# One DRAIN of GpSimd between the output scatters of a fused attention, MoE and routed-expert kernel

## The chip, the cores and the metric

The kernel runs on one core of a Trainium2 chip. The metric is the device time of one execution in microseconds; shown are the median of three runs and one profiled execution of the same program.

## The reference

Three stages follow each other, all in float32. The attention has 4 batches of 8 heads, 576 positions and 64 columns per head, with a bias made of a running sum. Its output, 2304 rows of 512, goes through a dense layer whose hidden value is the largest of three products. The last stage routes each row to one of 8 experts and writes the row of the result:

```python
    e_idx = np.argmax(logits, axis=1)
    ...
    for e in range(E):
        mask = e_idx == e
        ...
        h = np.maximum(x[mask] @ w1[e], 0.0)
        out[mask] = gate_w[mask, None] * (h @ w2[e])
```

## The kernel before

The change touches only the last stage, the routed experts. Its rows are cut into units of up to 256 rows of one expert. There are ten units in a fixed order, numbered 0 to 9 by `n` in the loop at line 811; unit 9 has 128 rows at most. Behind them stand eleven more units inside nested `tc.If(n_u > n)` (line 835 and on), which run only when the experts' row counts ask for them; with these inputs none does.

For each unit the weights of its expert are loaded by SyncE (`weights`), the rows are gathered by GpSimd with an indirect DMA (`gather`), turned and multiplied by TensorE (`transposed`, `stage_1`), and multiplied again 128 rows at a time (`stage_2(u, 0)` and `stage_2(u, 1)`). `stage_2` ends with ScalarE writing the scaled rows to `y` and GpSimd scattering them to their places in the output by an indirect DMA (line 661). Each such scatter writes the whole tensor `out` as the program sees it, so each waits until the one before has landed. Ten units make 19 scatters.

GpSimd issues four kinds of DMA in the whole program: the split of weights (line 127), the routing table's entries (line 506), the gathers (line 578) and the scatters (line 661).

Behind the last unit every engine loads the number of further units (line 832), branches past the nested blocks (line 833), and meets the others in the program's closing steps, which the profile puts on line 889. There GpSimd has a semaphore instruction for the blocks that were jumped over (INC_SWDGE_SEM), then a DRAIN, then a barrier that all five engines share, a clearing of semaphores and a second barrier. Each engine has DRAINs of its own in these closing steps, and each has one more at the program's start (line 882).

The order of instructions on each engine is set by a scheduler when the program is built. `tc.keep_in_program_order` holds an instruction at the place where the code has it.

Of the kernel before, what the change touches and what calls it, by code (L numbers as in the profile page):

```python
# [47 lines left out]
N_EARLY = 4  # L48

T_PE = T_EARLY  # L50
NU_STATIC = 5
# [34 lines left out]
def fused_kernel(tc, qk, vd, sd, w64, mod, wg, wgt, mb, we, cst, csi, out):  # L86
    nc = tc.nc
    V, A, G, P, SP = nc.vector, nc.scalar, nc.gpsimd, nc.tensor, nc.sync
    top = ExitStack()
    with top:  # L90
# [60 lines left out]
        with ExitStack() as es:  # L151
# [248 lines left out]
            for p in range(1, NP):  # L400
# [17 lines left out]
                if p % (H // 2) == H // 2 - 1:  # L418
                    b = PORD[p] // (H // 2)
                    n = 0  # L420
# [163 lines left out]
        def weights(u, n, which, raws):  # L584
            pools = SETS[(2 * n + which) % 3]
            hs, ls = [], []
            for g in range(4):
                pool, tag = pools[g]
                raw = raws[g % len(raws)].tile([128, 2, 512], F32, tag="raw", name="e_raw")
                SP.dma_start(out=raw.rearrange("p a n -> p (a n)"), in_=we[bass.ds(u["e"], 1), which * 4 + g].rearrange("e p n -> p (e n)"))  # L590
                for a in range(2):
                    h = pool.tile([128, 512], F32R, tag=tag, name="e_h")
                    lo = pool.tile([128, 512], F32R, tag=tag, name="e_l")
                    A.copy(out=h, in_=raw[:, a])  # L594
                    V.tensor_tensor(out=lo, in0=raw[:, a], in1=h.bitcast(F32), op=ALU.subtract)  # L595
                    hs.append(h)
                    ls.append(lo)
            u[which] = hs, ls

        def transposed(u):  # L600
            u["x"] = xt = xbp.tile([128, 2, 4, UNIT], F32R, tag="xb", name="x2t")[:, :, :, 0:u["n"]]
            for a in range(2):
                x_ps = ps_a.tile([128, 512], F32, tag="a", name="x_ps").rearrange("p (c n) -> p c n", c=2)[:, :, 0:u["n"]]
                for c in range(2):
                    for i in range(u["n"] // 128):
                        k = 2 * a + c
                        P.transpose(out=x_ps[:, c, i * 128:(i + 1) * 128], in_=u["g"][:, i, k * 128:(k + 1) * 128], identity=ident)
                A.copy(out=xt[:, 0, 2 * a:2 * a + 2], in_=x_ps)
                V.tensor_tensor(out=xt[:, 1, 2 * a:2 * a + 2], in0=x_ps, in1=xt.bitcast(F32)[:, 0, 2 * a:2 * a + 2], op=ALU.subtract)
# [41 lines left out]
        def stage_2(u, i):  # L651
            hs, ls = u[1]
            y_ps = ps_b.tile([128, DM], F32, tag="b", name="y_ps")
            cs = slice(i * 128, (i + 1) * 128)
            for f in range(NF2):
                P.matmul(y_ps, u["h"][:, f, cs], hs[f], start=f == 0, stop=False)  # L656
                P.matmul(y_ps, u["h"][:, f, cs], ls[f], start=False, stop=False)  # L657
                P.matmul(y_ps, u["l"][:, f, cs], hs[f], start=False, stop=f == NF2 - 1)  # L658
            y = x2p.tile([128, DM], F32, tag="x2", name="y")
            A.activation(out=y, in_=y_ps, func=ACTF.Copy, scale=u["m"][:, i, 1:2])  # L660
            G.indirect_dma_start(out=out[:, :], out_offset=bass.IndirectOffsetOnAxis(ap=u["m"].bitcast(I32)[:, i, 0:1], axis=0), in_=y[:, :], in_offset=None, bounds_check=T - 1, oob_is_err=False)  # L661
# [84 lines left out]
        def unit(n):  # L746
            if n >= N_EARLY:
                return prep_u(n - N_EARLY) if n < N_EARLY + NU_STATIC else prep_u(U, UNIT // 2)
            if n > 1:
                gather(early[n], T_EARLY * 128)  # L750
            return early[n]
# [63 lines left out]
        for n in range(N_EARLY + NU_STATIC + 1):  # L815
            if n:
                weights(u, n, 1, [rawp, raw2])
            nxt = None
            if n < N_EARLY + NU_STATIC:
                nxt = unit(n + 1)  # L820
                weights(nxt, n + 1, 0, [rawp, raw2])
            stage_2(u, 0)
            if nxt:
                transposed(nxt)
                if nxt["n"] == 128:
                    stage_1(nxt)
            if u["n"] > 128:
                stage_2(u, 1)
            if nxt and nxt["n"] > 128:
                stage_1(nxt)  # L830
            u = nxt
# [61 lines left out]
```

## Time and profile before

| | us |
|---|---|
| median of 3 runs | 765.94 (764.58 to 766.84) |
| profiled execution | 761.42 |
| its span, first to last instruction | 759.5 |
| mean granted TensorE clock, share of full | 0.987 |

The span is what the trace covers; 1.92 us of the profiled execution's time lie around it. An engine's name with a q behind it (POOLq, SPq) is the engine's instruction queue: semaphore instructions, branches and DRAINs are its, and do not count as busy time of the engine. POOL is GpSimd and SP is SyncE.

### The profile page before, as it was taken

The numbers are of one execution on the slowest core, as the hardware profiler recorded it, in microseconds if no ns is written. First come the engines' busy times: TensorE is split into PE (matmuls) and PEld (weight loads), VectorE is DVE, ScalarE is ACT, GpSimd is POOL, SyncE is SP. The second block draws the span as 40 slices with busy tenths as digits, with TensorE's granted clock in tenths as the row PEclk, the third lists the DMA queues.
The fourth block names the chain that finished last, engine by engine and source line by source line (L and its number), as shares of the span: only waits on it lengthen the run. The fifth ranks groups of instructions, "written<-read, shape, count | busy, mean of one in ns | idle before, by whom it ended". The sixth has DMA issues, their size and how long they took to land. (4 is left out here: it accounts for less than half of the span.)

```text
span 759.5 us, 13658 instructions
## 1 busy us (share of the span) xinstructions
PE 719.9 (95%) x4602; PEld 641.6 (84%) x4602; DVE 532.9 (70%) x1599; ACT 405.7 (53%) x976; POOL 178.7 (24%) x218
## 2 busy tenths in 40 slices
PE   4888999999999999999999999999999999999993
PEld 3666698778899799999999998989889998899982
DVE  6888888987767579593777796746785765656620
ACT  6886787876766445222222223535665755556620
POOL 6445554544321100001010111032221221221101
PEclk9998999999999999999999999999999999999997
DMA  7566655675421174101101101747557666566500
GB/s 219 159 225 185 209 159 184 184 227 145 135 69 62 33 280 145 40 15 22 43 22 52 45 25 50 250 153 236 199 152 262 222 197 246 189 245 213 189 15 18
DMA packets 45104, 108.56 MB, mean 143 GB/s; under 512 B 8992, under 2 KB 12992, under 8 KB 45024
## 3 DMA queue, kind: packets, MB, share of 16 engines
q1 hardware_dynamic: 37368, 90.75, 37.4%
q0 software_dynamic: 4912, 11.82, 4.8%
q10 hardware_dynamic: 2744, 5.02, 1.8%
q8 instruction: 38, 0.62, 0.3%
q14 instruction: 42, 0.34, 0.2%
HBM read 93.55 MB, written 12.18 MB: 139 GB/s over the span
## 5 line engine op out<-in xcount | busy, mean ns | idle before, releaser
L143 PE MATMUL a_ps<-xh,w_h 128*128 128x384 f32 (+2 forms) x492 | 159.5, 325 | 4.7 <-DVE h L323 3.7
L146 PE MATMUL a_ps<-xl,w_h 128*128 128x384 f32 (+2 forms) x492 | 158.1, 321 | 0.2 <-POOL xl L312 0.2
L147 PE MATMUL a_ps<-xh,w_l 128*128 128x384 f32 (+2 forms) x492 | 156.8, 319 | 0.0
L595 DVE TENSOR_TENSOR e_l<-e_raw,e_h 128x512 fp32r<-128x512 f32 x160 | 102.9, 688 | 16.8 <-ACT e_h L594 13.5
L246 ACT ACTIVATE e<-e,mn 128x64 f32<-128x64 f32 (+4 forms) x160 | 89.2, 559 | 29.7 <-DVE mn L244 29.4
L594 ACT CAST e_h<-e_raw 128x512 fp32r<-128x512 f32 x160 | 93.2, 624 | 21.4 <-DMA e_raw<-in_we 12.2
L143 PEld LDWEIGHTS a_ps<-xh,w_h 128*128 128x128 f32 x492 | 92.6, 188 | 7.2 <-DVE h L323 4.4
L146 PEld LDWEIGHTS a_ps<-xl,w_h 128*128 128x128 f32 x492 | 92.6, 188 | 0.8 <-POOL xl L312 0.4
L147 PEld LDWEIGHTS a_ps<-xh,w_l 128*128 128x128 f32 x492 | 92.5, 188 | 0.1
L242 PE MATMUL s_ps<-hl 128*128 128x64 f32 (+2 forms) x192 | 67.4, 363 | 16.2 <-DVE hl L213 9.0
L628 PE MATMUL h_ps<-x2t,e_h 128*128 128x256 f32 x288 | 81.0, 282 | 0.0
L629 PE MATMUL h_ps<-x2t,e_l 128*128 128x256 f32 x288 | 80.8, 282 | 0.0
L625 PE MATMUL h_ps<-x2t,e_h 128*128 128x256 f32 x288 | 79.9, 282 | 0.2 <-issue 0.2
L482 DVE CUSTOM_DVE_ANT_0 junk<-x,wg 128x512 bf16<-128x512 f32 x96 | 66.0, 687 | 17.2 <-ACT x L556 16.2
L506 POOL DMA_INDIRECT table<-meta,si x18 | 19.5, 1083 | 230.6 <-DVE mx L486 90.9
L275 PE MATMUL t_ps<-ident,e 128*128 128x128 f32 x480 | 70.7, 283 | 2.9 <-ACT pt L280 1.4
L244 DVE CUSTOM_DVE_ANT_0 e<-s_ps,mask 128x64 f32<-128x64 f32 (+4 forms) x160 | 63.2, 425 | 4.0 <-PE s_ps L243 2.9
L275 PEld LDWEIGHTS t_ps<-ident,e 128*128 128x128 f32 x480 | 58.1, 146 | 6.2 <-DVE pt L278 1.9
L656 PE MATMUL y_ps<-e_h,gh 128*128 128x512 f32 x152 | 61.3, 404 | 0.4 <-ACT gh L648 0.4
L243 PE MATMUL s_ps<-k_b,q_b 66*128 66x64 f32 (+2 forms) x192 | 60.4, 327 | 0.6 <-DMA k_b<-augk 0.6
L658 PE MATMUL y_ps<-e_h,gl 128*128 128x512 f32 x152 | 60.7, 399 | 0.0
L657 PE MATMUL y_ps<-e_l,gh 128*128 128x512 f32 x152 | 59.8, 394 | 0.0
(179 smaller groups left out, 1479.0 us busy)
## 6 DMA issues: line engine op xcount, KB each, us to landing
e_raw<-in_we SPq DMA_DIRECT2D x80, 512.0 KB
qk_r<-in_qk SPq DMA_DIRECT2D x30, 576.0 KB
w_raw<-in_w SPq DMA_DIRECT2D x24, 512.0 KB
v_r<-in_vd SPq DMA_DIRECT2D x16, 320.0 KB
rb<-r_d SPq DMA_DIRECT2D x32, 160.0 KB
x2d<-x ACTq DMA_DIRECT2D x18, 256.0 KB
w_h<-w_z POOLq DMA_DIRECT2D x9, 256.0 KB, 4.2
wg<-in_wg SPq DMA_DIRECT2D x4, 512.0 KB
```

The costliest lines, as they stand in the source:

```text
L143: ins = P.matmul(a_ps, wh[:, c], xh[:, c], start=c == 0, stop=False).ins
L146: P.matmul(a_ps, wh[:, c], xl[:, c], start=False, stop=False)
L147: P.matmul(a_ps, wl[:, c], xh[:, c], start=False, stop=c == 3)
L242: P.matmul(s_ps, hl[:, 1, q0:q0 + nq], hl[:, 0, k0:k0 + n], start=True, stop=False)
L246: ex = A.activation(out=ec, in_=ec, func=ACTF.Exp, bias=mn[0:nq, c:c + 1], scale=-1.0, accum_out=l[0:nq, c:c + 1]).ins
L275: last_t[0] = P.transpose(out=t_ps[:, n * 128:(n + 1) * 128], in_=e[:, EOFF[c] + kb * 128:EOFF[c] + (kb + 1) * 128], identity=ident).ins
L482: V.tensor_tensor_reduce(out=junk, in0=x2, in1=wg_sb[ei // 2][:, ei % 2, :], scale=1.0, scalar=0.0, op0=ALU.mult, op1=ALU.add, accum_out=l ...
L594: A.copy(out=h, in_=raw[:, a])
L595: V.tensor_tensor(out=lo, in0=raw[:, a], in1=h.bitcast(F32), op=ALU.subtract)
L625: ins = P.matmul(h_ps, w(hs, f, c), xt[:, 0, c], start=c == 0, stop=False).ins
L628: P.matmul(h_ps, w(hs, f, c), xt[:, 1, c], start=False, stop=False)
L629: P.matmul(h_ps, w(ls, f, c), xt[:, 0, c], start=False, stop=c == 3)
```

## The change

A DRAIN of GpSimd is put into the loop over units at `n == 7`, the last unit but two, behind `stage_2(u, 1)`, which issues that unit's second scatter.

```diff
             if u["n"] > 128:
                 stage_2(u, 1)
+            if n == N_EARLY + NU_STATIC - 2:
+                tc.keep_in_program_order(G.drain())
             if nxt and nxt["n"] > 128:
                 stage_1(nxt)
```

`N_EARLY` is 4 and `NU_STATIC` is 5. The built programs of before and after differ in this one instruction on GpSimd; the other four engines have the same instructions in the same order with the same waits. Lines behind the edit have numbers higher by two in the changed kernel.

This is GpSimd's order in the changed program from the last gather to the branch, with the semaphores that each waits for. The view does not list DRAINs. The first two scatters are unit 7's, the next two unit 8's, the last unit 9's.

```order
L578 DMA xg_9204<-x2d_73,mt_9202 128x512 [waits DMAHW0_49,Pool_49]
L661 DMA out_0<-y_8971,mt_8591 2304x512 [waits DMASW2_49,Activation_49]
L661 DMA out_0<-y_9016,mt_8591 2304x512 [waits DMASW4_49,Activation_49]
L661 DMA out_0<-y_9274,mt_8896 2304x512 [waits DMASW5_49,Activation_49]
L661 DMA out_0<-y_9361,mt_8896 2304x512 [waits DMASW7_49,DMASW6_49,Activation_49]
L661 DMA out_0<-y_9431,mt_9202 2304x512 [waits DMASW7_49,DMASW0_49,Activation_49]
L834 TENSOR_LOAD nt_i_6789 [waits DVE_49]
L835 COMPARE_AND_BRANCH
```

The new DRAIN stands between the third row and the fourth; nothing else moved. Before it GpSimd has issued all its DMAs but the last three scatters.

## Rows read from the trace of the kernel before

**Rows 1.** The page: the span, and each engine's busy time and share.

```profile
span 759.5 us, 13658 instructions
PE 719.9 (95%) x4602; PEld 641.6 (84%) x4602; DVE 532.9 (70%) x1599; ACT 405.7 (53%) x976; POOL 178.7 (24%) x218
```

**Rows 2.** Busy time by stretch of the end, with granted clock and DMA share.

```profile
core 0: us, PE busy (x) PEld busy (x) DVE busy (x) ACT busy (x) POOL busy (x), PEclk, DMA share, GB/s
...
713.00:720.00 7.00, 7.00 (x61) 7.00 (x60) 4.95 (x10) 4.10 (x11) 0.76 (x1) 1.00 0.62 211
720.00:729.00 9.00, 9.00 (x53) 7.72 (x52) 3.56 (x8) 3.23 (x8) 0.00 (x0) 1.00 0.01 3
...
753.00:759.50 6.50, 0.00 (x0) 0.00 (x0) 0.00 (x0) 0.00 (x0) 0.00 (x0) 0.50 0.00 0
```

**Rows 3.** Timeline of GpSimd, 690 to 760 us: start, duration, idle time before.

```profile
712.78 0.98 POOL L661 DMA_INDIRECT out<-y,mt  x1 [5.79 <-ACT y L660]
729.65 0.97 POOL L661 DMA_INDIRECT out<-y,mt  x1 [15.90 <-ACT x2t L608]
740.96 0.97 POOL L661 DMA_INDIRECT out<-y,mt  x1 [10.34 <-ACT y L660]
748.28 0.97 POOL L661 DMA_INDIRECT out<-y,mt  x1 [6.35 <-ACT y L660]
```

**Rows 4.** Line 833, 740 to 760 us: ns min/median/max, first and last start.

```profile
L833 POOLq EVENT_SEMAPHORE  x5: 17/42/43, 751.3 to 751.7; - x5
...
L833 POOLq COMPARE_BRANCH  x1: 53/53/53, 748.6 to 748.6; - x1
...
L833 POOLq INC_SWDGE_SEM  x1: 1500/1500/1500, 751.8 to 751.8; - x1
```

**Rows 5.** Line 889, the closing steps, 753 to 758.5 us alone.

```profile
L889 SPq EVENT_SEMAPHORE  x12: 28/28/28, 753.2 to 753.9; - x12
L889 SPq DRAIN  x2: 7/10/13, 754.0 to 754.0; - x2
L889 POOLq DRAIN  x1: 5377/5377/5377, 753.3 to 753.3; - x1
```

**Rows 6.** Line 889, all of the span.

```profile
L889 POOLq EVENT_SEMAPHORE  x4: 17/17/17, 758.7 to 759.4; - x4
L889 POOLq DRAIN  x3: 50/107/5377, 753.3 to 759.2; - x3
L889 SPq DRAIN  x3: 7/7/13, 754.0 to 758.9; - x3
...
L889 ACTq DRAIN  x2: 8/10/13, 750.6 to 758.9; - x2
```

**Rows 7.** Line 882, the program's start.

```profile
L882 POOLq INC_SWDGE_SEM  x1: 27/27/27, 0.1 to 0.1; - x1
...
L882 POOLq DRAIN  x1: 183/183/183, 0.3 to 0.3; - x1
```

**Rows 8.** GpSimd's instructions by line: the four kinds of DMA that it issues.

```profile
L578 POOL DMA_INDIRECT xg<-x2d,mt x19 | 19.9, 1048 | 39.1 <-DMA mt<-table 28.9 <-issue 9.5 <-POOL xg L576 0.7
L506 POOL DMA_INDIRECT table<-meta,si x18 | 19.5, 1083 | 230.6 <-DVE mx L486 90.9 <-DVE nm L494 83.8 <-DVE si L505 36.1
...
L661 POOL DMA_INDIRECT out<-y,mt x19 | 18.9, 992 | 77.1 <-ACT y L660 59.8 <-ACT x2t L608 16.4 <-issue 0.9
...
L127 POOL DMA_DIRECT2D w_h<-w_z x9 | 5.2, 582 | 6.6 <-DVE w_z L125 4.1 <-DVE x L300 1.7 <-DVE r L256 0.8
```

**Rows 9.** Waits of SyncE's queue, 740 to 760 us: total, times, longest.

```profile
SPq L889 <- PEq L889: 5.4, 2, 4.8
```

**Rows 10.** The page: DMA queues that carried instructions.

```profile
q8 instruction: 38, 0.62, 0.3%
q14 instruction: 42, 0.34, 0.2%
```

**Rows 11.** DMA packets between 752.6 and 759.5 us.

```profile
DMA packets 0, 0.00 MB, mean 0 GB/s; under 512 B 0, under 2 KB 0, under 8 KB 0
```

## The prediction

> **What bounds the kernel now.** I first read the page's busy shares: TensorE is busy 95% of the span [rows 1], so for nearly all of it only fewer or faster matmuls would help, and a GpSimd instruction is neither. The change must act where TensorE is not the bound, or not at all. So I went to the end of the span. The busy time by stretch [rows 2] shows that from 753 to 759.5 us no compute engine does anything and no DMA moves: 6.5 us in which only instruction queues work. What they do there is read from the closing steps, line 889. In the stretch 753 to 758.5 us [rows 5] SyncE passes twelve semaphores and two DRAINs and is done at 754.0; GpSimd has one single instruction, a DRAIN that starts at 753.3 and takes 5377 ns. The reader should then look at the whole line [rows 6]: GpSimd's first semaphore instruction of the barrier starts at 758.7, as that DRAIN ends (753.3 + 5.38 = 758.68), and everything behind it takes 759.5 - 758.7 = 0.8 us. SyncE's waits give the same time from the other side: its longest wait in the closing steps is 4.8 us [rows 9], and 754.0 + 4.8 = 758.8. The row names TensorE's queue as the releaser, but TensorE has nothing that long; the one long thing under way is GpSimd's DRAIN.
>
> So the last 11.2 us run: last scatter issued at 748.28 [rows 3], GpSimd's branch at 748.6 and its INC_SWDGE_SEM from 751.8 to 753.3 [rows 4], the DRAIN to 758.7, and 0.8 us of barriers. The DRAIN is nearly half of this, and all of it but the first 0.7 us is waited for by everyone.
>
> **What that DRAIN is made of.** GpSimd's other DRAINs take 183 ns at the program's start [rows 7] and 50 and 107 ns directly behind the long one (the two shorter of the three in [rows 6]). So a DRAIN of GpSimd is not long by itself. What differs is what GpSimd has done since the DRAIN before. Before the long one lie all its DMAs: 19 gathers, 18 table entries, 19 scatters and 9 weight splits, 65 in all [rows 8]; before each of the three short ones lies none. The long DRAIN does not wait for data, for no packet moves between 752.6 us and the end [rows 11], and not for the last scatter's instruction, which ended at 748.28 + 0.97 = 749.25 [rows 3], four microseconds before the DRAIN began. Nor does it wait for code, which comes as DMA packets of two queues [rows 10] and would be among the packets that are not there. What is left is work of GpSimd's own. I take it to be bookkeeping of its DMAs that is left until a DRAIN asks for it, in proportion to their number: (5377 - 183) / 65 = 80 ns to (5377 - 50) / 65 = 82 ns each, 81 in the sums below. This is the step that no row proves, since the trace has one long DRAIN and no second count to divide by.
>
> A page states the opposite of what could be gained here: by the Trainium skill, VectorE: DVE Perf Modes, section The DRAIN you can't avoid, the DRAINs in a program's opening and closing steps take about 12 ns, always, on all five engines. The trace agrees for SyncE (7 to 13 ns) and ScalarE (8 to 13 ns) [rows 6] and not for GpSimd, at 5377 ns; by the rule the end would hold nothing to save and the time would stay at 765.94.
>
> **The change, part by part.** It adds one DRAIN behind the scatter at 712.78 us and moves nothing.
>
> *The new DRAIN itself.* It comes up while that scatter is at work, so it can be done no earlier than 712.78 + 0.98 = 713.8. With 62 DMAs behind it I price it at 62 x 81 ns + 0.1 = 5.1 us, so it ends at about 719. Bounds: 50 ns (the shortest row) below; above, if it should also wait for that scatter's data, the DMA traffic of this stretch, which is heavy until 720 and gone after (share 0.62, then 0.01 [rows 2]), so 720 or a little later. What is queued behind it on GpSimd is unit 8's first scatter, which starts at 729.65 after 15.9 us of idle time and is held by ScalarE [rows 3]. That scatter also waits for the landing of the one before it, so a DRAIN that waits for the landing adds nothing there. No other engine waits for GpSimd in between: no gather or memset is left to issue. The cover is 15.9 us against 5.1, so I take the DRAIN at zero. If the cover were gone, every microsecond over 15.9 would push the scatter at 729.65; the one at 740.96 has 10.3 us of idle time of its own before it, so the end would not feel it until about 26 us.
>
> *The last DRAIN.* Three scatters lie between the new DRAIN and the last one: 3 x 81 ns + 0.1 = 0.35 us in place of 5.38. Bounds: 0.05 and 5.38 us. I take 0.35, because GpSimd's DRAINs with nothing before them are all near the lower bound. It then ends at 753.3 + 0.35 = 753.65, before SyncE's last DRAIN at 754.0. So SyncE becomes the last to arrive, and the exact length no longer matters as long as it is under 0.7 us. That also makes the result the same if the bookkeeping goes by packets or bytes and not by DMAs.
>
> *What is late next.* SyncE's semaphores pass from 753.2 to 754.0, and begin as INC_SWDGE_SEM ends (751.8 + 1.5 = 753.3). That instruction took 27 ns at the start [rows 7] and 1500 ns here. If its 1.5 us were part of the same bookkeeping they would shrink too, by up to 1.47 us, and SyncE would move with them. I take none of it, since it has eleven skipped blocks' semaphores to set here and nothing at the start, and keep 1.5 us as the far end.
>
> *The sum.* The barrier opens at 754.0 plus a handover of 0.05 to 0.1 (GpSimd's first semaphore instruction followed its DRAIN in less than 0.05), in place of 758.7: 4.6 us saved. The span becomes 759.5 - 4.6 = 754.9, the profiled execution 761.42 - 4.6 = 756.8. The three runs shown have a median of 765.94, 4.5 us above the profiled execution; the closing steps do not depend on what makes that difference, so I take the same 4.6 us off it: 761.3 us, 0.6% less.
>
> **Rivals.**
>
> *The long DRAIN has a fixed price once any DMA was issued.* It might ask each of the core's 16 DMA engines in turn, 5377 / 16 = 336 ns each, however many DMAs there were. For it: one long DRAIN cannot tell a fixed price from a proportional one, and the short ones all have no DMA before them. Against it: a fixed price would be large for so common an instruction. Then the new DRAIN costs 5.4 us inside 15.9 us of idle time, the last one still finds three scatters and costs 5.4 us, and the time stays at 765.94.
>
> *The DRAIN only waits until the engine is idle, and what it waits for lies behind the new one.* Then whatever ran from 753.3 to 758.7 began after 713 us, for instance with the last scatter, the branch or INC_SWDGE_SEM, and clearing the engine earlier saves nothing: 765.94. Against it: the last scatter's instruction was over by 749.25, and a scatter follows another's start within 7.3 us (740.96 to 748.28) without any such tail in between. The Trainium skill states this rule, in PSUM — Partial Sum Buffer, section Engine vs sequencer instructions: a drain waits for the engine to go fully idle. The trace neither shows what kept GpSimd from being idle nor excludes it.
>
> *The inserted instruction shifts GpSimd's code.* GpSimd's branch at 748.6 is followed by 2.7 us until its next instruction at 751.3 [rows 4], the first of the code behind the jump. Code comes in packets of 0.62 MB / 38 = 16 KB and 0.34 MB / 42 = 8 KB [rows 10]. If one more instruction pushes the code behind the branch across the edge of such a piece, a second fetch of 2.7 us comes on top. With a last DRAIN that stays long this makes 765.94 + 2.7 = 768.6, slower; with the gain it leaves 761.3 + 2.7 = 764.0. It decides the sign only together with a DRAIN that does not shrink by more than 2.7 us. Against it: the code must stand just at an edge for one instruction more to matter.
>
> **How the numbers follow.** A difference under 0.3%, 2.3 us, can't be told from no change here. Forecast, proportional bookkeeping: 0.80. Fixed price: 0.12. Idle rule: 0.05. Shifted code with no gain: 0.03. So faster 0.80, same 0.17, slower 0.03. The predicted time is 761.3. For the range: the runs shown reach 1.4 below and 0.9 above their median, and the profiled execution lies lower still; INC_SWDGE_SEM could give 1.5 more, so the low end is 761.3 - 1.4 - 1.5 = 758.4, and the high end 764.2, the forecast with the shifted code or with a last DRAIN that keeps half of its length (761.3 + 2.7 = 764.0), rounded up. The cases without a gain, 0.20 together, lie above it.
>
> **What would show it.** In the changed profile, line 830 has a GpSimd DRAIN from about 713 us of 4 to 7 us; the scatter behind it still starts near 729.65 and still waits for ScalarE; the first GpSimd DRAIN of line 891 takes under 0.7 us; SyncE's longest wait in the closing steps falls from 4.8 us to under 0.3; and from the issue of the last scatter to the end there are 6.6 us, not 11.2. The forecast is wrong if the DRAIN on line 891 is still 5 us (fixed price, or the idle rule, which the length of the one on line 830 tells apart: 5 us or 1 us), or if the steps between the branch and the DRAIN grow.

## The result, and the profile after

The changed kernel takes 758.08 us (median of 14 runs, 753.47 to 763.51) against 766.68 us of the kernel before (14 runs, 764.27 to 771.43): a ratio of 0.9887, 95% interval 0.9861 to 0.9913. It is faster, as forecast, by 8.6 us where 4.6 were forecast, and 0.3 us below the low end of the range. The profiled execution took 757.26 us.

The page of the changed kernel, with the span and the busy times that answer to [rows 1]:

```profile
span 755.4 us, 13659 instructions
PE 718.7 (95%) x4602; PEld 640.3 (85%) x4602; DVE 533.2 (71%) x1599; ACT 404.6 (54%) x976; POOL 179.4 (24%) x218
```

One instruction more, and the engines' work is the same. Now the new DRAIN, line 830 (lines behind the edit have numbers higher by two):

```profile
L830 POOLq DRAIN  x1: 9429/9429/9429, 714.2 to 714.2; - x1
```

And GpSimd's timeline from 714 us on, which answers to [rows 3]: start, duration, idle time before and its releaser.

```profile
714.48 0.97 POOL L661 DMA_INDIRECT out<-y,mt  x1 [5.79 <-ACT y L660]
731.36 0.98 POOL L661 DMA_INDIRECT out<-y,mt  x1 [15.90 <-ACT x2t L608]
742.67 0.97 POOL L661 DMA_INDIRECT out<-y,mt  x1 [10.33 <-ACT y L660]
750.00 0.97 POOL L661 DMA_INDIRECT out<-y,mt  x1 [6.36 <-ACT y L660]
```

The DRAIN ends at 714.2 + 9.4 = 723.6, nearly eight microseconds before the scatter behind it starts. The idle times of 15.90, 10.33 and 6.36 us are those of [rows 3] within 0.01, with the same releasers: nothing on GpSimd is held up. The whole stretch lies 1.7 us later than in the profile before, and the scatter ahead of the DRAIN does so already (714.48 against 712.78), so the DRAIN has no part in that.

The branch and what stands behind it, line 835, 740 to 760 us, which answers to [rows 4]:

```profile
L835 POOLq EVENT_SEMAPHORE  x5: 17/43/43, 753.1 to 753.4; - x5
...
L835 POOLq COMPARE_BRANCH  x1: 58/58/58, 750.3 to 750.3; - x1
...
L835 POOLq INC_SWDGE_SEM  x1: 260/260/260, 753.5 to 753.5; - x1
```

The closing steps, line 891, in the stretch 753 to 754.6 us alone, which answers to [rows 5]:

```profile
L891 SPq EVENT_SEMAPHORE  x12: 27/28/28, 753.7 to 754.4; - x12
L891 SPq DRAIN  x2: 7/10/13, 754.5 to 754.5; - x2
L891 POOLq DRAIN  x1: 294/294/294, 753.8 to 753.8; - x1
L891 POOLq EVENT_SEMAPHORE  x1: 17/17/17, 754.6 to 754.6; - x1
```

And SyncE's waits, 740 to 760 us, which answer to [rows 9]: total, times, longest.

```profile
SPq L891 <- PEq L891: 0.7, 2, 0.5
```

Two durations have changed. The DRAIN took 5377 ns in [rows 5] and takes 294 ns here: it ends at 754.1, SyncE's last DRAIN comes at 754.5, GpSimd passes the barrier at 754.6. So the way from the start of that DRAIN to the barrier fell from 758.7 - 753.3 = 5.4 us to 754.6 - 753.8 = 0.8 us: 4.6 us. And INC_SWDGE_SEM took 1500 ns in [rows 4] and takes 260 ns here: another 1.24 us. Together 5.84 us, and from the issue of the last scatter to the end it is 755.4 - 750.0 = 5.4 us in place of 759.5 - 748.28 = 11.2, the same 5.8. The branch with the pause behind it has not changed (750.3 to 753.1, before 748.6 to 751.3).

### The profile page after: what moved, and what is told of

It reads as the page before. It is cut to its first block, busy times and chain, and to the rows that moved or that the text cites. A ratio compares the mean times of both kernels' runs of the same rounds, so it can differ in the third digit from the quotient of the medians.

```text
span 755.4 us, 13659 instructions
## 1 busy us (share of the span) xinstructions
PE 718.7 (95%) x4602; PEld 640.3 (85%) x4602; DVE 533.2 (71%) x1599; ACT 404.6 (54%) x976; POOL 179.4 (24%) x218
## 3 DMA queue, kind: packets, MB, share of 16 engines
q0 software_dynamic: 4912, 11.82, 4.9%
## 5 line engine op out<-in xcount | busy, mean ns | idle before, releaser
L242 PE MATMUL s_ps<-hl 128*128 128x64 f32 (+2 forms) x192 | 67.0, 361 | 15.2 <-DVE hl L213 9.0
```

Source lines behind the costliest of these rows:

```text
L242: P.matmul(s_ps, hl[:, 1, q0:q0 + nq], hl[:, 0, k0:k0 + n], start=True, stop=False)
```

## The experiments

Twelve kernels, in three comparisons. In each, all kernels share the runs of the kernel before on the same chip (29, 23 and 21 runs, medians 766.83, 765.89 and 767.38). The first comparison ran on one chip, the second and third on another. The ratios below are as recorded for each comparison; they are not the ratios of these medians and can differ from them by up to 0.3% (drain_n8: 0.9888, where its medians give 0.9913). Three questions stand behind them: what the long DRAIN is made of, whether the place or the mere presence of an instruction matters, and where the gain beyond 5.8 us comes from.

**First comparison.** The kernel before, unchanged (control); the change once more (drain_n7); a memset in place of the DRAIN, on a column of a tile that nothing reads any more (memset_n7); and the DRAIN behind the last scatter, so that no DMA is left for the closing steps (drain_n9).

> The kernel before, unchanged, timed against itself. Both theories: a ratio of 1.000, within 0.3%. It shows how far runs of one kernel differ in time and granted clock, and so whether 8.6 us of measured gain can be more than the 5.9 us that the closing steps of the two profiles differ by.

> The changed kernel again. Theory A (the whole gain lies in the closing steps: last DRAIN 5.38 to 0.29 us, INC_SWDGE_SEM 1.50 to 0.26, 11.2 to 5.4 us from the last scatter's issue to the end): ratio 0.9923, 5.9 us, and spans equal to those of the control up to the last scatter. Theory B (the DRAIN also makes something ahead of the end faster, in this execution or in the next): 8 to 9 us again, ratio about 0.988, with the last scatter issued 2 to 3 us earlier than in the control.

```
+            if n == 7:
+                tc.keep_in_program_order(G.memset(took[:, 0:1], 0.0))
```

> A memset of one column of a tile that nothing reads any more, at the DRAIN's place, instead of the DRAIN: one more GpSimd instruction without a DRAIN. If the DRAIN's work on past DMAs is the cause: ratio 1.000, last DRAIN 5.4 us, INC_SWDGE_SEM 1.5 us as before. If it is a shift of GpSimd's code or any pause of GpSimd: a gain like the change's, 0.988 to 0.992.

```
+            if n == 9:
+                tc.keep_in_program_order(G.drain())
```

> The DRAIN behind the last scatter of unit 9 instead of unit 7, so with no DMA left after it and no idle time to hide in. Work per DMA: the new DRAIN takes about 5.4 us behind the last scatter, in the open, the one in the closing steps about 0.1 us, INC_SWDGE_SEM 0.3 us or less; the time is that of before or up to 2 us better, since the new DRAIN starts when the scatter is issued at 748 us and overlaps its 3 us of landing and the branch's 2.7 us only in part: ratio 0.996 to 1.000. If a DRAIN of any place sped up the end, 0.990.

Measured: control 765.80 us (12 runs), ratio 0.9983 (0.9954 to 1.0011). drain_n7 757.57 (6 runs), ratio 0.9887 (0.9854 to 0.9920), with the 294 and 260 ns of the change again and 5.6 us from the last scatter to the end. memset_n7 766.14 (12 runs), ratio 0.9998 (0.9967 to 1.0029). drain_n9 767.37 (12 runs), ratio 1.0008 (0.9982 to 1.0033).

In memset_n7, line 835 and line 891, 745 us to the end:

```profile
L835 POOLq INC_SWDGE_SEM  x1: 1500/1500/1500, 753.8 to 753.8; - x1
...
L891 POOLq DRAIN  x3: 50/107/5377, 755.3 to 761.3; - x3
```

An instruction more at the same place changes neither duration and gives no time: it is the DRAIN, and not one instruction more and a shift of the code behind it. In drain_n9, line 830, line 835 and line 891:

```profile
L830 POOLq DRAIN  x1: 6593/6593/6593, 750.3 to 750.3; - x1
...
L835 POOLq COMPARE_BRANCH  x1: 58/58/58, 757.5 to 757.5; - x1
L835 POOLq INC_SWDGE_SEM  x1: 183/183/183, 760.5 to 760.5; - x1
...
L891 POOLq DRAIN  x3: 34/47/107, 760.7 to 762.0; - x3
```

With no DMA left, the first closing DRAIN takes 47 ns and INC_SWDGE_SEM 183 ns. But the new DRAIN stands in the open: the branch starts at 757.5, 7.0 us behind the last scatter's start (0.3 us in control), and from the last scatter to the end it is 11.75 us (11.4 in control). The work isn't avoided. It is only worth moving to where GpSimd has nothing else to do.

**Second comparison.** The DRAIN behind unit 3's scatters, with 47 DMAs before it and 18 left (drain_n3, one run), to give the price per DMA a count in between. The other three follow a third theory about the gain beyond 5.8 us: TensorE idles through the closing steps, its clock falls there, and the next execution might begin slower for it; a shorter end would then give time twice. tail_pe adds 26 matmuls behind the last one to the kernel before, tail_long adds 32 memsets behind the last scatter to it, and n7_tail_pe adds 18 such matmuls to the changed kernel. Nothing reads what these matmuls and memsets write.

```
+            if n == 3:
+                tc.keep_in_program_order(G.drain())
```

> The DRAIN behind unit 3 instead of unit 7: 47 of the 65 DMAs lie before it, 18 after. From the three counts so far (0, 3 and 65 DMAs left: last DRAIN 0.047, 0.294 and 5.377 us; INC_SWDGE_SEM 0.183, 0.260 and 1.500 us) work per DMA is 82 and 20 ns, so the last DRAIN takes 0.047 + 18 x 0.082 = 1.52 us and INC_SWDGE_SEM 0.183 + 18 x 0.020 = 0.55 us. If the work goes by something else than the number of DMAs (bytes, or time since the last DRAIN: 200 us here against 35), the two come out more than 0.2 us away.

```
-            u = nxt
+            done, u = u, nxt
+        idle_ps = ps_b.tile([128, DM], F32, tag="b", name="idle_ps")
+        for k in range(26):
+            tc.keep_in_program_order(P.matmul(idle_ps, done["h"][:, k % NF2, 0:128], done[1][0][k % NF2], start=True, stop=True))
```

> The kernel before, without the DRAIN, with 26 matmuls behind the last one whose result nothing reads: TensorE is busy some 6 us longer in the closing steps, beside GpSimd's DRAIN, and idle about 6 us at the end in place of 12. The closing steps stay at 11.3 us. Theory C (what the change gains beyond its 5.8 us of closing steps, 2.8 us in 20 runs against 65, comes from less half-speed clock early in the next execution, because TensorE was idle for a shorter time at the end of this one): ratio 0.9963, about 764.1 us. Theory D (it has nothing to do with TensorE's idle time): ratio 1.000.

```
-            u = nxt
+            done, u = u, nxt
+        for k in range(32):
+            tc.keep_in_program_order(G.memset(done["g"][:, 0:1], 0.0))
```

> The kernel before with 32 memsets of a dead tile behind the last scatter, so that the closing steps, and TensorE's idle time in them, are some 10 us longer, about 22 us. Theory C (half a microsecond of slower front for each microsecond of idle TensorE at the end): the time grows by the closing steps' growth and 3 to 5 us more, so spans up to the last scatter grow too and the granted clock falls further than the longer idle end explains. Theory D: it grows by the closing steps' growth alone.

```
+            if n == 7:
+                tc.keep_in_program_order(G.drain())
...
+        for k in range(18):
+            tc.keep_in_program_order(P.matmul(idle_ps, done["h"][:, k % NF2, 0:128], done[1][0][k % NF2], start=True, stop=True))
```

> The change and 18 such matmuls behind the last one together: TensorE is idle about 2.5 us at the end in place of 6.6, the closing steps stay at 5.4 us. Theory C: 2 us less than the change alone, about 756.3, ratio 0.986. Theory D: the same as the change, 758.3, ratio 0.9887.

Measured: drain_n3 760.42 us (one run). Its line 830, line 835 and line 891:

```profile
L830 POOLq DRAIN  x1: 8451/8451/8451, 622.0 to 622.0; - x1
...
L835 POOLq INC_SWDGE_SEM  x1: 560/560/560, 755.6 to 755.6; - x1
...
L891 POOLq DRAIN  x3: 46/107/1519, 756.2 to 758.2; - x3
```

The closing steps took 1519 and 560 ns, where 1.52 and 0.55 us had been worked out from the counts beforehand. The prediction had left open whether the work goes by DMAs, packets or bytes. Queue q0 carries GpSimd's DMAs; this is the page's row of it in the kernel before (packets, MB, share):

```profile
q0 software_dynamic: 4912, 11.82, 4.8%
```

From 629 us to the end of drain_n3, behind its DRAIN, the same queue has 1440 packets and 4.20 MB. With 5330 ns (5377 - 47) for all of it, the 18 DMAs left in drain_n3 would cost 5330 x 4.20 / 11.82 = 1894 ns by bytes, 5330 x 1440 / 4912 = 1563 by packets and 5330 x 18 / 65 = 1476 by DMAs; measured are 1519 - 47 = 1472. So it goes by the number of DMAs.

The DRAIN on line 830 ends at 630.5, and it does hold something: the gather queued behind it.

```profile
622.25 1.00 POOL L661 DMA_INDIRECT out<-y,mt  x1 [4.29 <-ACT y L660]
631.33 1.04 POOL L578 DMA_INDIRECT xg<-x2d,mt  x1 [8.08 <-issue]
...
752.08 0.97 POOL L661 DMA_INDIRECT out<-y,mt  x1 [6.35 <-ACT y L660]
```

That gather starts 9.1 us after the scatter before it, where the kernels without a DRAIN at this place have 5.6 to 7.0. It delays nothing: from this scatter to the last one it is 752.08 - 622.25 = 129.8 us, and the same two scatters lie 129.8 to 129.9 us apart in all fourteen profiles, whether no DRAIN, one or (drain_all) six stand from the first of the two on.

tail_pe took 765.84 us (12 runs), ratio 0.9995 (0.9964 to 1.0025). The busy times, granted clock and DMA share of its last 12.5 us:

```profile
753.40:765.90 12.50, 6.23 (x28) 4.84 (x26) 0.00 (x0) 0.69 (x1) 0.97 (x1) 0.85 0.07 24
```

And those of the last 12.8 us of control:

```profile
749.60:762.40 12.80, 0.35 (x2) 0.00 (x0) 0.00 (x0) 0.69 (x1) 0.97 (x1) 0.72 0.06 22
```

TensorE is busy for 6.2 us of it instead of 0.35, and its mean granted clock there rises from 0.72 to 0.85; the time doesn't move. n7_tail_pe, with a granted clock of 1.00 to the end, took 761.48 us (12 runs), ratio 0.9935 (0.9909 to 0.9962): not better than the change alone. tail_long took 781.13 us (6 runs), ratio 1.0203 (1.0161 to 1.0245). Its GpSimd timeline from 748 us on:

```profile
748.64 0.97 POOL L661 DMA_INDIRECT out<-y,mt  x1 [6.39 <-ACT y L660]
749.60 18.58 POOL L833 MEMSET xg<- 128x512 f32 x32
```

From the last scatter to the end it is 776.8 - 748.6 = 28.2 us, 17.0 more than before, and the time rises by 781.13 - 765.89 = 15.2 us, where the third theory asked for 3 to 5 us more than the 17.0. A longer end costs no more than its own length. The third theory falls.

**Third comparison.** The change a third time (drain_n7_b), the DRAIN one unit later, with 64 DMAs before it and 1 left (drain_n8), a DRAIN behind each of the units 0 to 8 (drain_all), and the kernel before once more (control_b).

> The changed kernel a third time, since its two comparisons gave 8.7 us and the closing steps of the profiles differ by 5.8, while the change together with idle matmuls gave 5.0. Theory A2 (the gain is the closing steps' 5.8 us; the rest is the spread of the stages ahead, which differs by 1 to 3 us from one set of runs to the next): ratio near 0.9924 here, between 0.989 and 0.996. Theory B (there is a further gain of 2 to 3 us that belongs to the DRAIN): 0.9887 again.

```
+            if n == 8:
+                tc.keep_in_program_order(G.drain())
```

> The DRAIN one unit later, behind unit 8's second scatter: 64 DMAs before it, 1 after. Work per DMA: it takes 65 x 0.082 = 5.3 us from its scatter's start or more while that scatter lands, in 7.3 us between two scatters, so it just fits and delays the last scatter by 0 to 1 us; last DRAIN 0.13, INC_SWDGE_SEM 0.20 us, closing steps 5.4 us as with unit 7, because SyncE's semaphores set the end in both. Theory A2: 0.991 to 0.994; theory B: like the change, 0.988 to 0.990.

```
+            if n < 9:
+                tc.keep_in_program_order(G.drain())
```

> A DRAIN behind each of the units 0 to 8, so each has 2 to 4 DMAs' work except the first, which has 35. Work per DMA: the DRAINs are short where their scatter has landed, the closing steps are as with unit 8, and the time is that of the change (A2: 0.991 to 0.994; B: 0.988 to 0.990) unless one of the early DRAINs holds a gather, which TensorE waits for; then it is slower by what that wait adds.

> The kernel before, unchanged, beside itself once more: ratio 1.000; how far it is off shows how far one set of runs can be off by itself.

Measured: drain_n7_b 761.39 us (9 runs), ratio 0.9938 (0.9908 to 0.9968). drain_n8 760.73 (6 runs), 0.9888 (0.9849 to 0.9928). drain_all 761.56 (8 runs), 0.9925 (0.9890 to 0.9960). control_b 767.0 (12 runs), 0.9988 (0.9960 to 1.0015). The intervals of the first three overlap; none of these three kernels can be told from the others.

Line 830, line 835 and line 891 of drain_n8:

```profile
L830 POOLq DRAIN  x1: 6508/6508/6508, 747.0 to 747.0; - x1
...
L835 POOLq INC_SWDGE_SEM  x1: 203/203/203, 758.0 to 758.0; - x1
...
L891 POOLq DRAIN  x3: 46/107/131, 758.3 to 759.5; - x3
```

Its last two scatters, 7.33 us apart as without a DRAIN between them (748.28 - 740.96 = 7.32 in [rows 3]):

```profile
747.23 0.97 POOL L661 DMA_INDIRECT out<-y,mt  x1 [10.34 <-ACT y L660]
754.56 0.97 POOL L661 DMA_INDIRECT out<-y,mt  x1 [6.36 <-ACT y L660]
```

And line 830 of drain_all, where nine DRAINs stand:

```profile
L830 POOLq DRAIN  x9: 2585/6494/7047, 555.1 to 746.8; - x9
```

The ninth DRAIN of drain_all (746.8, 2585 ns) stands at the same place as the one of drain_n8, but with one DMA since the DRAIN before in place of 64: 2.6 us against 6.5. By the trace's semaphore records its scatter landed at 749.3, and the DRAIN ended at 749.4. In drain_n8 the scatter was issued at 747.23 and took 0.97 us; 64 x 82 + 47 = 5295 ns later is 753.5, and there the DRAIN ended (747.0 + 6.5). The same sum gives 756.9 for drain_n9, and 756.9 was measured. So, in these quiet stretches, a DRAIN behind a scatter lasts until that scatter has landed or until the count is worked off, whichever is later. In the busy stretches the sum doesn't hold: drain_n3's DRAIN would end at 622.25 + 1.00 + 47 x 0.082 + 0.05 = 627.2 by the count, its scatter landed at 628.5, and it ended at 630.5.

**What the closing steps cost, over all kernels.** GpSimd's DMAs since its DRAIN before, and the two durations in ns:

| kernel | DMAs | first closing DRAIN | INC_SWDGE_SEM |
|---|---|---|---|
| drain_n9 | 0 | 47 | 183 |
| drain_n8, drain_all | 1 | 131, 126 | 203, 203 |
| the change (3 profiles), n7_tail_pe | 3 | 294 | 260 |
| drain_n3 | 18 | 1519 | 560 |
| before, control, memset_n7, control_b, tail_pe, tail_long | 65 | 5377 | 1500 |

The DRAIN is 47 + 82 x N ns within 5 ns. INC_SWDGE_SEM is 200 + 20 x N ns from 3 DMAs on, and 17 ns less below.

**Where the gain beyond 5.8 us lies.** Each run has a span and a mean granted clock of TensorE, of which 1 is the higher level and 0.5 the lower. (1 - clock) x span is then an estimate of the time lost to the lower level, as if TensorE were the bound in those stretches, up to the clock's rounding (0.001, or 0.8 us). Taken off each run's time, it leaves about what the run would be without them. Means over the runs, us, with the standard error of the mean (drain_n3, with one run, and the kernels with matmuls or memsets behind the last unit are left out, since their closing steps differ from both the change's and those of before; chip 1 is the first comparison's, chip 2 that of the others):

| kernel | chip | runs | time | lost | rest |
|---|---|---|---|---|---|
| before, first comparison | 1 | 29 | 767.3 | 12.5 (0.5) | 754.8 (0.4) |
| before, second | 2 | 23 | 765.8 | 11.1 (0.6) | 754.7 (0.4) |
| before, third | 2 | 21 | 767.0 | 12.6 (0.6) | 754.4 (0.3) |
| control | 1 | 12 | 766.0 | 12.2 (0.8) | 753.8 (0.5) |
| control_b | 2 | 12 | 766.6 | 11.5 (0.9) | 755.1 (0.5) |
| memset_n7 | 1 | 12 | 766.5 | 11.9 (0.6) | 754.6 (0.9) |
| drain_n9 | 1 | 12 | 767.3 | 13.3 (0.7) | 754.0 (0.5) |
| the change, 14 runs of the result | not on record | 14 | 758.4 | 7.0 (1.0) | 751.4 (0.4) |
| drain_n7 | 1 | 6 | 758.0 | 6.7 (0.7) | 751.3 (0.6) |
| drain_n7_b | 2 | 9 | 761.7 | 9.5 (0.7) | 752.2 (0.7) |
| drain_n8 | 2 | 6 | 759.4 | 7.5 (1.6) | 751.9 (0.6) |
| drain_all | 2 | 8 | 761.3 | 9.5 (1.1) | 751.8 (0.4) |

The rest falls from about 754.6 (753.8 to 755.1) to about 751.7 (751.3 to 752.2), by 2.9 us: that is half of the 5.8 us, since the closing steps run at a granted clock of 0.5 and their other half is booked as lost. By them alone the lost time would fall by the same 2.9 us, from about 12.1 to 9.2. In drain_n7_b and drain_all it does (9.5, and the gain is 5.2 to 5.7 us), and the three kernels of the third comparison together, 23 runs, lose 9.0 (0.6) and gain 6.0 (0.8); in the result's set and in drain_n7 the lost time is 2 to 2.5 us lower still. So what goes beyond 5.8 us is less time at TensorE's lower clock, in some sets and not in others.

## Why the prediction was right or wrong

*The bound and the place.* Right: the kernel before was held at its end by GpSimd's queue, and 5.8 of the 8.6 us came from there.

*What the DRAIN is made of.* Right, and now shown: 82 ns for each DMA of GpSimd since its last DRAIN, where 80 to 82 had been worked out from one long and three short DRAINs. Counts of 0, 1, 3, 18 and 65 lie on one line. What the work consists of stays open; "bookkeeping" is only a name for it. The rule of the Trainium skill in VectorE: DVE Perf Modes, section The DRAIN you can't avoid (about 12 ns, on all engines) doesn't hold for GpSimd, at 34 to 5377 ns in the closing steps here.

*The rivals.* A fixed price would have left 5.4 us for three DMAs, and 294 ns were left. The idle rule would have made an early DRAIN useless. What the Trainium skill states in PSUM — Partial Sum Buffer, section Engine vs sequencer instructions (a drain waits until the engine is idle) fits the ninth DRAIN of drain_all, which ends 0.1 us behind its scatter's landing; in drain_n8 the DRAIN goes on for 4 us after that landing (749.5 to 753.5), so the landing is not all that it waits for; whether GpSimd is idle meanwhile the trace doesn't show. The shifted code is not what happened: in the changed kernel the pause behind the branch is as long as before (2.8 and 2.7 us), and memset_n7, with one instruction more at the same place, has a ratio of 0.9998.

*The new DRAIN.* Forecast at 4 to 7 us, 5.1 in the sum, with an end at 720 "or a little later" at most; measured at 9.4 us with an end at 723.6. Mis-sized, and without effect, since 15.9 us covered it. The sum that fits drain_n8 and drain_n9 gives 714.48 + 0.97 + 62 x 0.082 + 0.05 = 720.6 here, 3 us short. The place differs by its DMA traffic. From 713 to 720 us of the changed kernel, and behind it (columns as in [rows 2]):

```profile
713.00:720.00 7.00, 7.00 (x60) 7.00 (x60) 5.25 (x11) 5.03 (x12) 0.97 (x1) 1.00 0.87 279
720.00:729.00 9.00, 9.00 (x58) 8.09 (x57) 4.47 (x9) 3.39 (x8) 0.00 (x0) 1.00 0.02 8
...
753.00:755.40 2.40, 0.00 (x0) 0.00 (x0) 0.00 (x0) 0.00 (x0) 0.00 (x0) 0.50 0.01 3
```

The DMA engines are busy for 0.87 of the first stretch, the scatter's first packet starts only at 717.6, 3.2 us after its issue (1.5 us in drain_n8), and the scatter landed at 721.1. With three DMAs to count, the same place still took 7.0 us (drain_all, the longest of nine), and that DRAIN ended 0.2 us behind its scatter's landing; with 62 it ended 2.6 us behind it. That traffic slows the DRAIN there is argued, not shown: no run took the traffic away.

*The last DRAIN, and what is late next.* Right: 0.35 us forecast, 0.29 measured; SyncE is the last to arrive; the barrier opens 0.1 us behind it; 4.6 us forecast for this step and 4.6 measured. SyncE's longest wait is 0.5 us, not under 0.3 as forecast, which costs nothing.

*The step that failed.* "I take none of it": INC_SWDGE_SEM's 1.5 us were put down to the skipped blocks' semaphores, and its part of the gain was kept only as the far end. It goes by the same count, 20 ns for each DMA, and it stands ahead of SyncE's last steps, so all that it loses comes off the end: 1.24 us. That is why 5.4 us are left from the last scatter's issue to the end and not the 6.6 that were forecast. The term was mis-sized at zero. Its two rows had told as much as the DRAIN's: 27 ns at the start with no DMA before it, 1500 ns at the end with 65 [rows 4, 7]. One argument (short without DMAs, long with them) was accepted for the one instruction and refused for the other.

*The rest of the miss.* With that term the forecast would have been 761.3 - 1.2 = 760.1, and a saving of 5.8 us, a ratio of 0.9924, which lies in the intervals of drain_n7_b, drain_n8, drain_all and n7_tail_pe, just outside drain_n7's and further outside that of the result (0.9861 to 0.9913). The other 2 to 3 us are less time at the lower clock (the table above). The low end of the range allowed 1.4 us for the spread of runs, from three runs; the medians of the changed kernel itself went from 757.57 to 761.39 in three sets. What isn't settled is why two of its sets lost so little time to the lower clock. In the profiles the stretches at the lower clock lie between 47 and 93 us, near 170, between 516 and 554 and at the very end, and the DRAIN stands at 714 us, so it cannot act on the earlier ones in the same execution. Behind it nothing differs up to the last scatter: 750.00 - 714.48 = 35.5 us, and 748.28 - 712.78 = 35.5 in [rows 3]. Acting on the next execution by way of TensorE's idle time was the third theory, which fell; no run tried another way. The front of the profiled executions isn't shorter with the DRAIN either: the last scatter is issued at 749.1 to 754.6 us in seven profiles with a hidden DRAIN (mean 751.8) and at 748.3 to 754.8 in seven without (mean 751.0). The intervals of the change's three sets just overlap (0.9861 to 0.9913, 0.9854 to 0.9920, 0.9908 to 0.9968), so chance between sets would do. The chip is a rival that was not tested: drain_n7 and drain_n7_b are the same kernel on two chips, and the sets of the second chip together gain no more than the closing steps give. Neither is shown.

## What to carry to other kernels

Look at what an engine's queue does after the last data has moved: a DRAIN or a semaphore instruction of microseconds there may be work that an earlier DRAIN could have done in an idle stretch. Where GpSimd issues many DMAs, one DRAIN in a pause long enough to hold it (6 to 10 us here), behind most of them, takes that work off the end; the exact place matters little as long as few DMAs are left, and at the very end it gains nothing. When one argument is used to price an instruction, apply it to every instruction that shows the same pair of rows.

## What was not expected of the hardware

INC_SWDGE_SEM, too, goes by the DMAs that GpSimd has issued since its last DRAIN: 183 ns with none, 260 with 3, 560 with 18, 1500 with 65. A DRAIN behind a running scatter waits for its landing even with few DMAs to count (2.6 us with one in a quiet stretch, 7.0 us with three in a busy one), so the nine of drain_all came to 53 us of DRAINs in all. Yet they cost nothing that can be seen: the scatters from unit 3 to the end lie as far apart as without them, and the ratio is 0.9925. And with the work unchanged, the time that a run loses to TensorE's lower clock differs between sets of the changed kernel by nearly 3 us (6.7 on one chip, 9.5 on another), which is more than the 2.3 us that a measurement was taken to tell apart.
